# The score maxima of an attention kernel: TensorE transposes in the first batch, block transposes after it, and the reduced maximum kept in PSUM

## The chip, the core and the metric

The kernel runs on one core of a Trainium2 chip. The metric is device time in microseconds (us) of one execution; less is better. Before the change the median of three runs is 1071.49 us (1071.37 to 1074.14).

Five engines work side by side and each executes its own instructions strictly in the order written: TensorE (PE; its weight loads have a row of their own, PEld), VectorE (DVE), ScalarE (ACT), GpSimd (POOL) and SyncE (SP, which here issues most DMAs). They wait for one another by semaphores.

## The reference

Hashed attention, then a two-layer feed-forward block, all in float32.

```
q_bits = (q @ proj > 0); k_bits likewise; buckets are the 6 bits read as a number
scores = where(q_bucket == k_bucket, 0.125 * q @ k.T, -1e9)      # 4 batches x 8 heads, 768 x 768, head dim 64
scores = scores - max(scores, axis=-1)                            # the part that the change touches
attn   = exp(scores);  attn = attn / (attn.sum(-1) + 1e-9)
x      = (attn @ v) gathered to 3072 x 512
h = x @ w_in (512 x 2048);  g = s * max(h, 0)**2 + b;  out = g @ w_out (2048 x 512)
```

## The kernel before, in words

A *slot* is one chunk of 256 queries of one head: 4 batches x 8 heads x 3 chunks = 96 slots. In a slot, TensorE writes the transposed scores (keys on the partitions, queries along the free axis) into three PSUM banks, 0 to 2 in one kind of slot and 5 to 7 in another. Slots of the first batch alternate between the two sets of banks. From the 25th slot on all slots use banks 0 to 2, since banks 5 to 7 then belong to the feed-forward block (`moe`), whose matmuls (L710 and L727) fill TensorE between the attention steps. The feed-forward work is added from the last slot of the first batch on (GATE = 23), so the first batch has none of it. Instead its 32 weight tiles are decoded there (`decode`: L362 and L363 on ACT, L364 and L365 on DVE, L366, L373 and L374 on POOL). Half of the heads of the first batch are computed in plain float32 (the *exact* ones), all others from operands split into two parts.

The maximum over the keys runs across the partitions and takes this chain in every slot, `scores` from L575 to L592:

1. L575, DVE: maximum over the six key tiles, three PSUM banks to `mx` (128x256, in SBUF).
2. L577, DVE: `mx` is transposed in place in blocks of 32x32.
3. L578, DVE: maximum over each block's 32 columns, to `nmt` (128x8).
4. L582, PE: transpose of `nmt` into PSUM bank 4 (8x128).
5. L584, DVE: maximum over the four groups of 32, negated, to `qm` (8x32, in SBUF).
6. L592, DVE, the *row operation*: `qm` repeated eight times, times eight columns of the identity, to 8x256 in SBUF (`zhl` in exact heads, `bq` in the others). Both its inputs are in SBUF.
7. L601 (exact) or L603, PE, six matmuls: they add the negated maximum to the scores in PSUM. Then ACT takes exp (L608).

PSUM bank 4 is shared by this chain and by all preparation of later heads: transposes L436 and L450, hash matmuls L469 and L479 to L481, sums of v L516 and L531.

No instruction order is written by hand. The code adds steps to a `Plan`, each with its engine, a cost in us, what it reads and writes, and a priority. `Plan.order` then simulates the engines with these costs and emits each engine's instructions in the order that came out. `plan.hold(4)` keeps bank 4 for one group of steps until the last of them is done. A cost is thus a planning number: it decides what stands between two steps, not how long they take.

Of the kernel before, what the change touches and what calls it, by code (L numbers as in the profile page):

```python
# [10 lines left out]
F32 = mybir.dt.float32  # L11
# [146 lines left out]
CHAIN = 0.05  # L158
OFF = 0.4
BEHIND = 8.0  # L160
LOOK = {DVE: 0.5, ACT: 0.0, POOL: 0.0}


@with_exitstack
def lsh_attention_moe(ctx: ExitStack, tc, q, k, v, proj, w_in, w_out, s, b, out):
# [31 lines left out]
    def tile_(name, shape, dt=F32):  # L197
        return const.tile(shape, dt, name=name)
# [13 lines left out]
    def act(n, fn, r, w, pr, more=0.0):  # L212
        plan.add(ACT, 0.13 + n / 1070.0 + more, fn, r, w, pr)
# [31 lines left out]
    zhl = tile_("zhl", [P, 2, CH], F32R)  # L245
    zpb = tile_("zpb", [P, NXP, CH])
    vmn = tile_("vmn", [D, 2 * H])
    nmt = tile_("nmt", [P, NR])
    QM = tile_("qm", [NR, SQ])
    oner = tile_("oner", [P, P], F32R)  # L250
    xpb = tile_("xpb", [P, NXP, CH])
    xsb = tile_("xsb", [P, 2, CH], F32R)
# [87 lines left out]
    def decode(u, pr):  # L340
# [9 lines left out]
        def raw():  # L350
            return box["t"]
# [10 lines left out]
        act(512, lambda: nc.scalar.activation(g, raw()[:, :, 1].bitcast(F32), AF.Copy, scale=float(2.0**-112)), rk + [("pace", u % PACE)], [gk], pr)  # L362
        act(512, lambda: nc.scalar.activation(raw()[:, :, 0], raw()[:, :, 0].bitcast(U32), AF.Copy, scale=float(2.0**-29)), rk, rk, pr)  # L363
# [190 lines left out]
    def scores(i, pr):  # L554
# [8 lines left out]
        for p in range(NP_):  # L563
# [5 lines left out]
                        continue  # L569
                    nc.tensor.matmul(o, ks[0:HR + NR, 0, kt], aq[0:HR + NR, cs], start=m == 0, stop=m == 1, skip_group_check=True)  # L570
            pe(mmc(CH, 8 if exact else 2), lead, AK(x) + KK(x) if exact else AK(x, g=CG[c])  + KK(x, (0, 2, 4)), [("b", pb[p])], pr, True)
        t, tk, nm, nk = MX, "mx", nmt, "nm"

        sc = bank[:, b0:b0 + NP_].rearrange("p b (m n) -> p n b m", n=CH)
        dve(S * TPC, lambda: nc.vector.tensor_reduce(t, sc, AX.XY, ALU.max), [("b", b) for b in pb], [tk], pr, 1.75)  # L575
        m2, m2k = MX, "mx"
        dve(CH, lambda: nc.vector.transpose(out=m2, in_=t), [tk], [m2k], pr, 0.33)  # L577
        dve(CH, lambda: nc.vector.tensor_reduce(nm, m2.rearrange("p (b n) -> p b n", n=SQ), AX.X, ALU.max), [m2k], [nk], pr, 0.33)  # L578
        plan.hold(4)
        plan.soon[len(plan.steps) - 1] = plan.now[1]  # L580
# [33 lines left out]
    def values(i, pr, pieces):  # L614
# [7 lines left out]
        for p in range(NP_):  # L622
            z, y = PIECES[i][p], nhl[0] % NHL
            nhl[0] += 1
            if not exact:
                act(512, lambda z=z, y=y: nc.scalar.copy(HL[2 * y].rearrange("p (m n) -> p m n", n=CH), pairs(z)), [("e", z)], [("hl", 2 * y)], pr)  # L626
# [12 lines left out]
            for p_ in pieces[(p * len(pieces) + NP_ - 1) // NP_:((p + 1) * len(pieces) + NP_ - 1) // NP_]:  # L639
                p_(i, pr + PP)  # L640
# [194 lines left out]
```

## Time and profile before

| | before |
|---|---|
| median of three runs | 1071.49 us |
| the profiled execution | 1071.43 us |
| its span, first to last instruction | 1069.6 us |
| PE busy | 1014.5 us (95%) |
| DVE busy | 731.7 us (68%) |
| ACT busy | 672.5 us (63%) |
| POOL busy | 659.8 us (62%) |
| mean granted TensorE clock | 0.986 |

Busy time is the union of an engine's instruction spans, so a matmul stretched by a slow clock counts in full. A stage is judged by its own idle time, not by these means: the first batch (to 193 us), the three batches that share TensorE with the feed-forward block (to about 890 us), and a tail with the feed-forward block alone.

### The profile page before, as it was taken

The numbers are of one execution on the slowest core, as the hardware profiler recorded it, in microseconds if no ns is written. First come the engines' busy times: TensorE is split into PE (matmuls) and PEld (weight loads), VectorE is DVE, ScalarE is ACT, GpSimd is POOL, SyncE is SP. The second block draws the span as 40 slices with busy tenths as digits, with TensorE's granted clock in tenths as the row PEclk, the third lists the DMA queues.
The fourth block names the chain that finished last, engine by engine and source line by source line (L and its number), as shares of the span: only waits on it lengthen the run. The fifth ranks groups of instructions, "written<-read, shape, count | busy, mean of one in ns | idle before, by whom it ended". The sixth has DMA issues, their size and how long they took to land.

```text
span 1069.6 us, 18187 instructions
## 1 busy us (share of the span) xinstructions
PE 1014.5 (95%) x6614; PEld 901.3 (84%) x6614; DVE 731.7 (68%) x940; ACT 672.5 (63%) x1325; POOL 659.8 (62%) x596
## 2 busy tenths in 40 slices
PE   8988869879999999999999999999999999999998
PEld 6876657768888988888888899888899889999997
DVE  6898998967788878878788778878778863000000
ACT  4767676757766666667766766676776765333332
POOL 1656777686677667767686677767776765222221
PEclk9999998979999999999999999999999999999999
DMA  6666655412332242234143233233242211101010
GB/s 175 148 185 155 176 150 130 139 30 71 103 96 65 59 120 60 69 94 120 32 114 86 68 106 95 64 91 90 60 118 65 64 40 50 60 1 59 8 43 20
DMA packets 93681, 93.07 MB, mean 87 GB/s; under 512 B 62744, under 2 KB 66328, under 8 KB 93592
## 3 DMA queue, kind: packets, MB, share of 16 engines
q1 hardware_dynamic: 88392, 74.87, 26.2%
q10 hardware_dynamic: 5200, 17.05, 5.5%
q8 instruction: 52, 0.85, 0.3%
q14 instruction: 37, 0.30, 0.1%
HBM read 48.24 MB, written 18.87 MB: 63 GB/s over the span
## 4 chain that ended last, share of the span: by engine, by line
PE 50%; DVE 7%; ACT 2%; POOL 1%; issue 1%; DMA 1%; DVEq 0%; SPq 0%; ACTq 0%; POOLq 0%
PE bank L710 18%; PE bank L727 17%; PE bank L603 4%; PE bank L570 3%; PE bank L634 2%; PE bank L633 2%; DVE bq L592 2%; DVE mx L575 1%; DVE zpb L673 1%; PE bank L661 1%; ACT et L608 1%; PE bank L450 1%; POOL glb L718 1%; DVE zb L653 1%; DVE qm L584 0%
## 5 line engine op out<-in xcount | busy, mean ns | idle before, releaser
L627 POOL TENSOR_TENSOR hl<-et,hl 128x512 fp32r<-128x512 f32 x216 | 279.4, 1319 | 103.5 <-ACT hl L626 80.6
L710 PE MATMUL bank<-xc,w 128*128 128x256 f32 x2304 | 329.6, 284 | 0.8 <-ACT rb L715 0.8
L710 PEld LDWEIGHTS bank<-xc,w 128*128 128x128 f32 x2304 | 303.2, 191 | 7.7 <-ACT rb L715 1.2
L727 PE MATMUL bank<-w,ghb 128*128 128x512 f32 x768 | 254.9, 399 | 0.0
L718 POOL TENSOR_TENSOR glb<-rb,ghb 128x512 fp32r<-128x512 f32 x96 | 127.8, 1331 | 136.4 <-ACT ghb L717 127.5
L653 DVE TENSOR_REDUCE zb<-et 128x256 f32<-128x1536 f32 x72 | 126.1, 1752 | 75.2 <-ACT et L608 73.9
L608 ACT ACTIVATE et<-bank 128x512 f32<-128x512 f32 x240 | 132.5, 625 | 68.3 <-PE bank L603 54.5
L575 DVE TENSOR_REDUCE mx<-bank 128x256 f32<-128x1536 f32 x96 | 168.0, 1750 | 7.8 <-PE bank L570 3.8
L727 PE MATMUL bank<-w,glb 128*128 128x512 f32 x384 | 152.9, 399 | 0.0
L715 ACT ACTIVATE rb<-bank 128x512 f32<-128x512 f32 x96 | 57.2, 596 | 149.4 <-PE bank L710 148.2
L727 PEld LDWEIGHTS bank<-w,ghb 128*128 128x128 f32 x768 | 135.4, 189 | 17.9
L626 ACT CAST hl<-et 128x512 fp32r<-128x512 f32 x216 | 130.9, 663 | 0.4
L633 PE MATMUL bank<-hl,vs 128*128 128x256 f32 x432 | 116.8, 290 | 4.6 <-DVE xpb L668 4.1
L634 PE MATMUL bank<-hl,vs 128*128 128x256 f32 x432 | 115.7, 287 | 3.8 <-POOL hl L627 3.8
L570 PE MATMUL bank<-aq,ks 84*128 84x256 f32 x504 | 104.6, 299 | 0.2 <-ACT et L608 0.2
L603 PE MATMUL bank<-bq,ks 128*128 128x256 f32 x504 | 83.2, 302 | 16.5 <-DVE bq L592 16.2
L735 DVE SCALAR_TENSOR_TENSOR osb<-bank,misc,bcs 128x512 f32<-128x512 f32 x22 | 16.0, 744 | 120.7 <-PE bank L727 120.6
L603 PEld LDWEIGHTS bank<-bq,ks 128*128 128x128 f32 x504 | 67.6, 194 | 30.9 <-DVE bq L592 28.6
L634 PEld LDWEIGHTS bank<-hl,vs 128*128 128x128 f32 x432 | 83.5, 193 | 10.5 <-POOL hl L627 5.6
L633 PEld LDWEIGHTS bank<-hl,vs 128*128 128x128 f32 x432 | 83.4, 193 | 10.4 <-DVE xpb L668 4.5
L570 PEld LDWEIGHTS bank<-aq,ks 84*128 84x128 f32 x504 | 82.6, 192 | 7.9 <-ACT et L608 1.2
L666 ACT ACTIVATE xpb<-bank,vmn 64x256 f32<-64x256 f32 x96 | 44.9, 468 | 70.0 <-PE bank L634 68.6
(117 smaller groups left out, 1613.7 us busy)
## 6 DMA issues: line engine op xcount, KB each, us to landing
xd<-xsb SPq DMA_DIRECT2D x48, 256.0 KB
xc<-xd SPq DMA_DIRECT2D x48, 256.0 KB
raw<-in_moe_w_in_dram ACTq DMA_DIRECT2D x16, 512.0 KB
raw<-in_moe_w_out_dram ACTq DMA_DIRECT2D x16, 512.0 KB
nat<-in_q_dram SPq DMA_DIRECT2D x32, 192.0 KB
nat<-in_k_dram SPq DMA_DIRECT2D x32, 192.0 KB
out_dram<-osb SPq DMA_DIRECT2D x22, 256.0 KB
ks<-aq SPq DMA_DIRECT2D x28, 192.0 KB
```

Of the source, the lines that this page charges most:

```text
L570: nc.tensor.matmul(o, ks[0:HR + NR, 0, kt], aq[0:HR + NR, cs], start=m == 0, stop=m == 1, skip_group_check=True)
L575: dve(S * TPC, lambda: nc.vector.tensor_reduce(t, sc, AX.XY, ALU.max), [("b", b) for b in pb], [tk], pr, 1.75)
L603: nc.tensor.matmul(o, ks[:, 1, kt], bq[:, cs], start=False, stop=m == 1, skip_group_check=True)
L608: act(512, lambda p=p, z=z: nc.scalar.activation(et(z) if plain(i) else pairs(z), bank[:, pb[p]] if plain(i) else bank[:, pb[p]].rearrange ...
L626: act(512, lambda z=z, y=y: nc.scalar.copy(HL[2 * y].rearrange("p (m n) -> p m n", n=CH), pairs(z)), [("e", z)], [("hl", 2 * y)], pr)
L627: pool(512, lambda z=z, y=y: nc.gpsimd.tensor_tensor(HL[2 * y + 1].rearrange("p (m n) -> p m n", n=CH), pairs(z), f32(HL[2 * y]).rearrange ...
L633: nc.tensor.matmul(av, VS[x][:, kt], HL[2 * y][:, ms], start=(kt == 0), stop=False)
L634: nc.tensor.matmul(av, VS[x][:, kt], HL[2 * y + 1][:, ms], start=False, stop=(kt == NT - 1))
L653: dve(S * TPC, lambda: nc.vector.tensor_reduce(ZB, es, AX.XY, ALU.add), [("e", z) for z in range(NE)], ["zb"], pr, 1.75)
L710: nc.tensor.matmul(hp, wt[("wi", n, cc)][:, m % 2, fs], xc[:, m // 2, :], start=(cc == 0 and m == 0), stop=(cc == NC_ - 1 and m == 2))
L718: pool(2 * CH, lambda r=r, gh=gh, gl=gl: nc.gpsimd.tensor_tensor(gl, r, f32(gh), ALU.subtract), [rk, hk], [lk], MP)
L727: nc.tensor.matmul(bank[:, 6 + t, :], (gh, gh, gl)[n][:, ts], wt[("wo", f)][:, n % 2], start=(f == 0 and n == 0), stop=(f == NF - 1 and n ...
```

## The change: what it does

In slots of the first batch (`turn` false) the block transposes and the reduction behind them are replaced. TensorE transposes `mx` as two 128x128 pieces into bank 4 (L588 after the change), one DVE reduction from PSUM takes the negated maximum (L590, 128x2, into its own half of `nmt`, which was cleared once), TensorE transposes that (L592), and the row operation (L599) reads bank 4 directly; there is no `qm` step.

In the other three batches (`turn` true) steps 1 to 4 stay, but the small maximum (L595 after the change) is written to free columns of bank 4 and the row operation (L599) reads it there. In all slots the row operation now has one input in PSUM and one in SBUF, and bank 4 is held until the row operation is done.

Several planning costs are changed: the block transpose from 0.33 to 0.45 us, the reductions from 0.33 to 0.42 and 0.26 to 0.27, the row operation from 0.33 to 0.41, and 0.05 or 0.06 more for ACT's decode steps and casts. So the order of all engines changes.

```diff
+TURN = 1
-    nmt = tile_("nmt", [P, NR])
-    QM = tile_("qm", [NR, SQ])
+    nmt = tile_("nmt", [P, 2, NR])
+    nc.vector.memset(nmt, 0.0)
@@ decode
-        act(512, ... AF.Copy, scale=float(2.0**-112)), rk + [("pace", u % PACE)], [gk], pr)
+        act(512, ... AF.Copy, scale=float(2.0**-112)), rk + [("pace", u % PACE)], [gk], pr, 0.06)
...
@@ scores
-        t, tk, nm, nk = MX, "mx", nmt, "nm"
+        turn = slots[i][0] >= TURN
+        t, tk, nm, nk = MX, "mx", nmt[:, turn], ("nm", turn)
...
-        dve(CH, lambda: nc.vector.transpose(out=m2, in_=t), [tk], [m2k], pr, 0.33)
-        dve(CH, lambda: nc.vector.tensor_reduce(nm, m2.rearrange("p (b n) -> p b n", n=SQ), AX.X, ALU.max), [m2k], [nk], pr, 0.33)
+        if turn:
+            dve(CH, lambda: nc.vector.transpose(out=t, in_=t), [], [tk], pr, 0.45)
+            dve(CH, lambda: nc.vector.tensor_reduce(nm, t.rearrange("p (b n) -> p b n", n=SQ), AX.X, ALU.max), [tk], [nk], pr, 0.42)
         plan.hold(4)
         plan.soon[len(plan.steps) - 1] = plan.now[1]
+        if not turn:
+            def across():
+                for j in range(TPC):
+                    nc.tensor.transpose(out=bank[:, 4, j * P:(j + 1) * P], in_=t[:, j * P:(j + 1) * P], identity=ident)
+            pe(0.23, across, [tk], [("b", 4, "c")], pr, True)
+            dve(CH, lambda: nc.vector.tensor_reduce(nm[:, 0:TPC], bank[:, 4, 0:CH].rearrange("p (j n) -> p j n", j=TPC), AX.X, ALU.max, negate=True), [("b", 4, "c")], [nk], pr, 0.41)
         pe(0.115, lambda: nc.tensor.transpose(out=bank[0:NR, 4, 0:P], in_=nm, identity=ident), [nk], [("b", 4, "c")], pr, True)
-        qm, qk = QM, "qm"
-        dve(CH, lambda: nc.vector.tensor_reduce(qm, bank[0:NR, 4, 0:P].rearrange("b (k n) -> b n k", n=SQ), AX.X, ALU.max, negate=True), [("b", 4, "c")], [qk], pr, 0.26)
-        plan.hold(None)
+        n, o = (NR, bank[0:NR, 4, P:P + SQ]) if turn else (TPC, bank[0:NR, 4, 0:P])
+        if turn:
+            dve(CH, lambda: nc.vector.tensor_reduce(o, bank[0:NR, 4, 0:P].rearrange("b (k n) -> b n k", n=SQ), AX.X, ALU.max, negate=True), [("b", 4, "c")], [("qm", 4)], pr, 0.27)
         def rows():
-            o = qm.rearrange("p (j n) -> p j n", j=1).broadcast_to([NR, NR, SQ])
-            d = ident[0:NR, 0:NR].rearrange("p (j n) -> p j n", n=1).broadcast_to([NR, NR, SQ])
-            nc.vector.scalar_tensor_tensor(mr.rearrange("p (j n) -> p j n", j=NR), o, -FLOOR, d, ALU.min, ALU.mult)
-        dve(CH, rows, [qk], [mk], pr, 0.33)
+            d = ident[0:NR, 0:n].rearrange("p (j n) -> p j n", n=1).broadcast_to([NR, n, CH // n])
+            nc.vector.scalar_tensor_tensor(mr.rearrange("p (j n) -> p j n", j=n), o.rearrange("p (j n) -> p j n", j=1).broadcast_to([NR, n, CH // n]), -FLOOR, d, ALU.min, ALU.mult)
+        dve(CH, rows, [("b", 4, "c"), ("qm", 4)], [mk], pr, 0.41)
+        plan.hold(None)
```

What this does to the order is shown at two places. The first is TensorE in the 46th slot (second batch), from the transpose of `nmt` to the six matmuls that need the row operation. `hl` and `vs` are the attention weights and values, `xc`, `w`, `ghb` and `glb` the feed-forward operands. Before:

```order
L582 MATMUL bank<-ident,nmt 8x128
L710 MATMUL bank<-xc_2_0_2463,w_756 128x256
L710 MATMUL bank<-xc_2_1_3322,w_798 128x256 x2
L633 MATMUL bank<-hl_1595,vs_3056 128x256
L634 MATMUL bank<-hl_1607,vs_3056 128x256
L633 MATMUL bank<-hl_1595,vs_3056 128x256
L634 MATMUL bank<-hl_1607,vs_3056 128x256
L710 MATMUL bank<-xc_2_1_3322,w_798 128x256
L603 MATMUL bank<-bq_71,ks_73 128x256 x6
```

And the same place in the changed kernel, where the transpose is L592 and the six matmuls are L611:

```order
L592 MATMUL bank<-ident,nmt 8x128
L735 MATMUL bank<-w_913,ghb 128x512
L641 MATMUL bank<-hl_1593,vs_3106 128x256
L642 MATMUL bank<-hl_1602,vs_3106 128x256
L641 MATMUL bank<-hl_1593,vs_3106 128x256
L642 MATMUL bank<-hl_1602,vs_3106 128x256
L735 MATMUL bank<-w_913,glb 128x512
L718 MATMUL bank<-xc_2_0_2399,w_1044 128x256
L611 MATMUL bank<-bq_71,ks_73 128x256 x6
```

Between the transpose and the matmuls that wait stood eight matmuls of 256 columns; now there are five of 256 and two of 512 columns, one 256-column matmul's worth more.

The second place is in the first batch, the thirteenth slot. TensorE before, from the transpose of `nmt`; `eqa` and `eka` are the exact queries and keys, `nat` the raw ones of a later head:

```order
L568 MATMUL bank<-eqa,eka 128x256 x4
L582 MATMUL bank<-ident,nmt 8x128
L450 MATMUL bank<-ident,nat_66 128x128 x3
L601 MATMUL bank<-zhl,oner 128x256 x6
L631 MATMUL bank<-et,eva 128x256 x2
```

And in the changed kernel, where L588 is the transposes of `mx`, L592 that of `nmt` and L609 the matmuls that need the row operation:

```order
L588 MATMUL bank<-ident,mx 128x128 x2
L639 MATMUL bank<-ex_86,vs_210 128x256
L639 MATMUL bank<-ex_87,vs_210 128x256 x2
L569 MATMUL bank<-eqa,eka 128x256 x2
L592 MATMUL bank<-ident,nmt 8x128
L569 MATMUL bank<-eqa,eka 128x256 x2
L609 MATMUL bank<-zhl,oner 128x256 x2
L517 MATMUL bank<-misc,vs_780 64x1 x6
L609 MATMUL bank<-zhl,oner 128x256 x4
```

The chain now passes TensorE twice, with five matmuls between the two passes and two behind the second. The next head's preparation (L450) no longer stands between the transpose and the matmuls that need the row operation.

## Rows read from the trace of the kernel before

**Rows 1.** The page: span, and busy time of each engine.
```profile
span 1069.6 us, 18187 instructions
PE 1014.5 (95%) x6614; PEld 901.3 (84%) x6614; DVE 731.7 (68%) x940; ACT 672.5 (63%) x1325; POOL 659.8 (62%) x596
```

**Rows 2.** Busy time by stage: first batch, passage, three batches, tail.
```profile
core 0: us, PE busy (x) PEld busy (x) DVE busy (x) ACT busy (x) POOL busy (x), PEclk, DMA share, GB/s
16.70:193.00 176.30, 153.20 (x819) 124.81 (x818) 157.11 (x222) 121.97 (x244) 111.44 (x95) 0.96 0.59 159
193.00:260.00 67.00, 58.66 (x357) 51.36 (x356) 53.53 (x64) 43.47 (x89) 51.40 (x45) 0.87 0.28 75
260.00:890.00 630.00, 613.11 (x4253) 555.10 (x4252) 502.31 (x610) 441.75 (x888) 446.78 (x409) 1.00 0.30 82
890.00:1069.60 179.60, 176.06 (x1116) 159.11 (x1114) 10.10 (x14) 59.86 (x99) 46.85 (x39) 1.00 0.09 32
```

**Rows 3.** Who waited for whom, PE, 260 to 890 us: total, times, longest.
```profile
PE bank L603 <- DVE bq L592: 13.5, 29, 0.9
PE bank L634 <- POOL hl L627: 3.1, 5, 0.9
```

**Rows 4.** The row operation and its kin: count, shortest/median/longest ns.
```profile
L592 DVE SCALAR_TENSOR_TENSOR bq<-qm,ident x84: 411/562/1579, 60.7 to 884.8; 8x256 fp32r<-8x256 f32 x84
L592 DVE SCALAR_TENSOR_TENSOR zhl<-qm,ident x12: 411/414/1200, 20.3 to 190.9; 8x256 fp32r<-8x256 f32 x12
L365 DVE SCALAR_TENSOR_TENSOR osb<-osb,raw x32: 628/691/1668, 24.1 to 224.1; 128x512 int32<-128x512 int32 x32
L668 DVE TENSOR_TENSOR xpb<-xpb,bank x72: 422/424/427, 209.0 to 895.9; 64x256 f32<-64x256 f32 x72
L741 DVE SCALAR_TENSOR_TENSOR osb<-bank,misc,bcs x4: 476/480/487, 1065.2 to 1066.5; 128x256 f32<-128x256 f32 x4
```

**Rows 5.** Timeline, one slot of the second batch: start us, us, instruction.
```profile
433.77 0.28 DVE L584 TENSOR_REDUCE qm<-bank 8x32 f32<-8x128 f32 x1 [0.77 <-PE bank L582]
434.09 1.58 DVE L592 SCALAR_TENSOR_TENSOR bq<-qm,ident 8x256 fp32r<-8x256 f32 x1
434.13 1.26 POOL L718 TENSOR_TENSOR glb<-rb,ghb 128x512 fp32r<-128x512 f32 x1
435.72 0.98 PE L603 MATMUL bank<-bq,ks 128*128 128x256 f32 x6 [0.94 <-DVE bq L592]
```

**Rows 6.** Row operations' busy time (count) by stage: first batch, passage, three batches.
```profile
16.70:193.00 176.30, 16.14 (x24) 0.96 0.59 159
193.00:260.00 67.00, 3.80 (x6) 0.87 0.28 75
260.00:890.00 630.00, 48.86 (x66) 1.00 0.30 82
```

**Rows 7.** Groups of the whole run: busy, mean ns, idle before.
```profile
L577 DVE STREAM_TRANSPOSE mx<-mx 128x256 f32<-128x256 f32 x96 | 42.6, 444 | 3.0
L578 DVE TENSOR_REDUCE nmt<-mx 128x8 f32<-128x256 f32 x96 | 40.3, 420 | 3.3
L582 PE MATMUL bank<-ident,nmt 128*8 128x128 f32 x96 | 26.5, 276 | 6.8 <-DVE bq L454 5.5 <-DVE nmt L578 0.7 <-DVE nat L484 0.4
L584 DVE TENSOR_REDUCE qm<-bank 8x32 f32<-8x128 f32 x96 | 25.6, 267 | 30.9 <-PE bank L582 29.8
```

**Rows 8.** Timeline: three TensorE transposes in a row.
```profile
417.58 0.49 PE L450 MATMUL bank<-ident,nat 128*128 128x128 f32 x3
```

**Rows 9.** Chain that ended last: start us, us; a feed-forward run of each kind.
```profile
899.45 2.87 PE bank L710 x24
902.32 2.77 PE bank L727 x12
```

**Rows 10.** Who waited for whom, PE, first batch (16.7 to 193 us).
```profile
PE bank L582 <- DVE bq L454: 5.3, 2, 4.4
PE bank L450 <- DVE qm L584: 4.3, 7, 1.5
PE bank L436 <- DVE qm L584: 2.3, 3, 1.7
PE bank L601 <- DVE zhl L592: 2.2, 5, 0.7
PE bank L516 <- DVE qm L584: 2.1, 2, 1.3
PE bank L603 <- DVE bq L592: 2.0, 3, 0.9
```

**Rows 11.** Timeline: the 25th maximum reduction; the longest stall of the passage.
```profile
192.92 1.68 DVE L575 TENSOR_REDUCE mx<-bank 128x256 f32<-128x1536 f32 x1
226.23 0.58 PE L633 MATMUL bank<-hl,vs 128*128 128x256 f32 x1 [4.11 <-DVE xpb L668]
```

More of the change, by code (lines that the diff above doesn't have):

```diff
@@ L361, in decode @@
         plan.add(ACT, 0.1, lambda: nc.scalar.dma_start(raw(), src.rearrange("p (n t) -> p n t", t=2)), KK("a") if u < PACE else [], rk + [("pace", u % PACE)], pr - 5, 5.0)
-        act(512, lambda: nc.scalar.activation(g, raw()[:, :, 1].bitcast(F32), AF.Copy, scale=float(2.0**-112)), rk + [("pace", u % PACE)], [gk], pr)
-        act(512, lambda: nc.scalar.activation(raw()[:, :, 0], raw()[:, :, 0].bitcast(U32), AF.Copy, scale=float(2.0**-29)), rk, rk, pr)
+        act(512, lambda: nc.scalar.activation(g, raw()[:, :, 1].bitcast(F32), AF.Copy, scale=float(2.0**-112)), rk + [("pace", u % PACE)], [gk], pr, 0.06)
+        act(512, lambda: nc.scalar.activation(raw()[:, :, 0], raw()[:, :, 0].bitcast(U32), AF.Copy, scale=float(2.0**-29)), rk, rk, pr, 0.06)
         dve(256, lambda: nc.vector.tensor_scalar(raw()[:, :, 1], gi, -2**31, None, ALU.bitwise_and), [gk], rk, pr, 0.6)
@@ L571, in scores @@
             pe(mmc(CH, 8 if exact else 2), lead, AK(x) + KK(x) if exact else AK(x, g=CG[c])  + KK(x, (0, 2, 4)), [("b", pb[p])], pr, True)
-        t, tk, nm, nk = MX, "mx", nmt, "nm"
+        turn = slots[i][0] >= TURN
+        t, tk, nm, nk = MX, "mx", nmt[:, turn], ("nm", turn)
         sc = bank[:, b0:b0 + NP_].rearrange("p b (m n) -> p n b m", n=CH)
         dve(S * TPC, lambda: nc.vector.tensor_reduce(t, sc, AX.XY, ALU.max), [("b", b) for b in pb], [tk], pr, 1.75)
-        m2, m2k = MX, "mx"
@@ L577, in scores @@
-        dve(CH, lambda: nc.vector.transpose(out=m2, in_=t), [tk], [m2k], pr, 0.33)
-        dve(CH, lambda: nc.vector.tensor_reduce(nm, m2.rearrange("p (b n) -> p b n", n=SQ), AX.X, ALU.max), [m2k], [nk], pr, 0.33)
+        mk = ("mrow", y) if exact else ("mr", x, c)
+        mr = zhl[0:NR, y] if exact else bq[0:NR, cs]
+        if turn:
+            dve(CH, lambda: nc.vector.transpose(out=t, in_=t), [], [tk], pr, 0.45)
+            dve(CH, lambda: nc.vector.tensor_reduce(nm, t.rearrange("p (b n) -> p b n", n=SQ), AX.X, ALU.max), [tk], [nk], pr, 0.42)
@@ L579, in scores @@
         plan.hold(4)
         plan.soon[len(plan.steps) - 1] = plan.now[1]
-        pe(0.115, lambda: nc.tensor.transpose(out=bank[0:NR, 4, 0:P], in_=nm, identity=ident), [nk], [("b", 4, "c")], pr, True)
-        qm, qk = QM, "qm"
-        dve(CH, lambda: nc.vector.tensor_reduce(qm, bank[0:NR, 4, 0:P].rearrange("b (k n) -> b n k", n=SQ), AX.X, ALU.max, negate=True), [("b", 4, "c")], [qk], pr, 0.26)
-        plan.hold(None)
-        mk = ("mrow", y) if exact else ("mr", x, c)
-        def rows():
-            mr = zhl[0:NR, y] if exact else bq[0:NR, cs]
-            o = qm.rearrange("p (j n) -> p j n", j=1).broadcast_to([NR, NR, SQ])
-            d = ident[0:NR, 0:NR].rearrange("p (j n) -> p j n", n=1).broadcast_to([NR, NR, SQ])
-            nc.vector.scalar_tensor_tensor(mr.rearrange("p (j n) -> p j n", j=NR), o, -FLOOR, d, ALU.min, ALU.mult)
@@ new lines, in scores, with rows @@
+        pe(0.115, lambda: nc.tensor.transpose(out=bank[0:NR, 4, 0:P], in_=nm, identity=ident), [nk], [("b", 4, "c")], pr, True)
+        n, o = (NR, bank[0:NR, 4, P:P + SQ]) if turn else (TPC, bank[0:NR, 4, 0:P])
+        if turn:
+            dve(CH, lambda: nc.vector.tensor_reduce(o, bank[0:NR, 4, 0:P].rearrange("b (k n) -> b n k", n=SQ), AX.X, ALU.max, negate=True), [("b", 4, "c")], [("qm", 4)], pr, 0.27)
+        def rows():
+            d = ident[0:NR, 0:n].rearrange("p (j n) -> p j n", n=1).broadcast_to([NR, n, CH // n])
+            nc.vector.scalar_tensor_tensor(mr.rearrange("p (j n) -> p j n", j=n), o.rearrange("p (j n) -> p j n", j=1).broadcast_to([NR, n, CH // n]), -FLOOR, d, ALU.min, ALU.mult)
@@ L625, in values @@
             if not exact:
-                act(512, lambda z=z, y=y: nc.scalar.copy(HL[2 * y].rearrange("p (m n) -> p m n", n=CH), pairs(z)), [("e", z)], [("hl", 2 * y)], pr)
+                act(512, lambda z=z, y=y: nc.scalar.copy(HL[2 * y].rearrange("p (m n) -> p m n", n=CH), pairs(z)), [("e", z)], [("hl", 2 * y)], pr, 0.05)
                 pool(512, lambda z=z, y=y: nc.gpsimd.tensor_tensor(HL[2 * y + 1].rearrange("p (m n) -> p m n", n=CH), pairs(z), f32(HL[2 * y]).rearrange("p (m n) -> p m n", n=CH), ALU.subtract), [("e", z), ("hl", 2 * y)], [("hl", 2 * y + 1)], pr, 1.3)
```

## The prediction

> **What bounds the kernel now.** I read the page first: span 1069.6 us, PE busy 1014.5 us of it, DVE next with 731.7 [rows 1]. So the time is TensorE's work plus TensorE's idle time, and the question is where that idle time lies. The table by stage tells it [rows 2]. In the first batch PE is busy 153.2 of 176.3 us (23.1 idle), in the passage to 260 us 58.7 of 67.0 (8.3 idle), in the three batches beside the feed-forward block 613.1 of 630.0 (16.9 idle), and in the tail 176.1 of 179.6. The feed-forward work is a filler that TensorE always has from 260 us on: an idle microsecond that goes there comes off the end, since the tail is TensorE work without a break.
>
> Then the waits of the third stage: 13.5 of its 16.9 us of idle time are one wait, L603 for the row operation L592, 29 times, 0.9 us at the longest [rows 3]. What the row operation takes is in its list of durations: 411 ns at the shortest, 562 in the middle, 1579 at the longest, for always the same 8x256 elements [rows 4]. The timeline shows what it waits for: at 434.09 it starts, GpSimd's L718 starts at 434.13 and ends at 435.39, and the row operation ends 0.28 us after that; L603 had stood idle for 0.94 us [rows 5]. The kin in the same list split alike. L365, also with two inputs in SBUF, spreads from 628 to 1668 ns. L668 and L741, with one input in PSUM, spread by 5 and 11 ns [rows 4]. So the spread goes with two SBUF inputs beside a running GpSimd instruction. In the first batch DVE is busy 157.1 of 176.3 us, more than PE [rows 2], and its longest waits of PE are for DVE or for bank 4 that DVE holds [rows 10].
>
> **Part 1: the row operation reads PSUM, all 96 slots.** Its busy time is 16.14 + 3.80 + 48.86 = 68.8 us, 0.717 us each [rows 6]. With one PSUM input I expect no spread. From below 0.411 us, the shortest of today; from above 0.480 us, L741 with three operands at the same 256 columns; I take 0.425, since L668, with one PSUM input and 256 columns, has 0.424 [rows 4]. That makes 96 x 0.425 = 40.8 us, 28 us less on DVE (22.7 to 29.3).
>
> L668 reads PSUM and takes 13 ns more than the undisturbed row operation reading SBUF [rows 4]. [...]
>
> On the path: the saving counts where PE waits. In the third stage the row operation costs 48.86 - 66 x 0.425 = 20.8 us more than it will, 0.32 us per slot, but PE waits in 29 slots only, for 13.5 us, on average 0.47 us [rows 3, 6]. At least 29 x 0.32 = 9.2 us go, if the waits were spread like the average slot; at most all 13.5. I take 12: the slots that wait are those with the long row operation, and the order now has one more 256-column matmul in front of L611, 2.87/24 = 0.12 us [rows 9]. What is late next is the chain from the transpose itself: 0.276 for L582, 0.267 for the reduction [rows 7], 0.425 and some 0.1 of handing over are 1.07 us, against 5 x 0.12 + 2 x 0.231 = 1.06 us of matmuls in the order after [rows 9]. In the first batch the same wait is 2.2 + 2.0 us [rows 10], of which 3.5 go. Part 1 gives -12 - 3.5 = **-15.5 us** (-11 to -18).
>
> **Part 2: the small maximum written to PSUM (72 slots).** No row shows a DVE write to PSUM. From below the reduction stays at 0.267 us; from above it costs as much more as the dearest PSUM reading above, 0.48 - 0.41 = 0.07 us, 5 us of DVE in 72 slots, of which PE sees what its order does not cover. I take 0: DVE idles 128 of 630 us in the third stage [rows 2]. Bank 4 is held 0.43 us longer per slot; behind it queue the preparation steps of later heads, and PE has feed-forward matmuls to put there. If that cover is gone, 0.43 us in each of the 72 slots would be 31 us; the order above shows it is not.
>
> **Part 3: the first batch (24 slots).** DVE loses the block transpose, its reduction and the small maximum, 0.444 + 0.420 + 0.267 = 1.13 us, and gains a reduction of 128x256 from PSUM. No row shows that one; from below 0.420 as from SBUF, from above 0.48 as L741; I take 0.42, for L668 shows 13 ns for PSUM. So DVE does 0.71 x 24 = 17 us less, and with the row operation (16.14 - 24 x 0.425 = 5.9) 23 us less of its 157. PE gains 48 transposes. Three in a row take 0.49 us, the first 0.27, so each further one 0.11 [rows 8, 7]: 48 x 0.11 = +5.3 us, all inside a stage in which PE idles 23.1 us. It also gains a wait: PE's second transpose waits for the DVE reduction in the middle of the chain. Behind it on PE's queue are the scores and values of neighbouring slots, for which ACT waits. Transposes, hand-over and reduction are 0.27 + 0.11 + 0.1 + 0.42 = 0.9 us, and in the order five matmuls of the exact kind stand between; I take the wait as covered on average.
>
> What does the lighter DVE buy? Between two bounds: if DVE sets the pace, the stage shortens by the 17 us that part 1 has not counted; if PE does, it gets 5.3 us longer. PE's waits other than for the row operation that end with DVE or bank 4 are 5.3 + 4.3 + 2.3 + 2.1 = 14 us in the first batch [rows 10]. I let three quarters go, for the preparation transposes no longer stand between the transpose and L609 in the order shown, and DVE is a seventh lighter: -10.5 + 5.3 = **-5 us** (-17 to +5).
>
> **Part 4: the costs.** They move instructions and remove none. The stalls that a new order may make or remove are of the size of the 4.11 us wait for L668 [rows 11]. The granted clock was 0.87 on average in the passage with that stall and 0.96 in the first batch, and 1.00 afterwards [rows 2]; 13% of 67 us and 4% of 176 us lost at half speed are 9 + 7 = 16 us. I take 0 with 8 to either side.
>
> Sum: 1071.4 - 15.5 - 5 = **1051 us**, against the profiled execution's own 1071.43, which is 0.06 below the median of the runs.
>
> **Rivals.**
>
> *The second pass over TensorE (slower).* In the first batch each chain stands twice in PE's queue. If neither the order's matmuls cover the first pass nor the second, each slot loses the pass and the reduction, 0.38 + 0.42 = 0.8 us; 24 slots make 19, the transposes 5.3, and the preparation that waits for bank 4 (4.3 + 2.3 + 2.1 = 8.7 us today [rows 10]) doubles: +33 - 15.5, 1089 us. It decides the sign from 0.4 us exposed per slot on (15.5 - 5.3 = 10 us over 24 slots). Half-way it is 1078. For it: PE is 87% busy there and already waits for bank 4. Against: the matmuls between the two passes, and DVE's 23 us.
>
> *The row operation does not get shorter.* If it waits for something other than GpSimd's use of SBUF, or PSUM costs as much, only part 3 is left: 1066 us. For it: rows 5 show one case and not the mechanism. Against: the two kin that never spread.
>
> *The clock.* [...] The granted clock fell in both stages in which PE had stalls of over 4 us [rows 2, 10, 11]. One more loses the stall and 9 us: 1051 + 13 = 1064 us. [...]
>
> *DVE sets the pace of the first batch.* Then 23 us go there in all, with 12 in the third stage: 1071.4 - 35 = 1036 us. For it: DVE is the busiest engine there. Against: PE at 87% with 5.3 us more.
>
> **How the numbers follow.** The forecast has 0.57, the second pass 0.09, the unshortened row operation 0.08, the clock 0.11, DVE's pace 0.15. The likeliest case gives 1051. The range runs from DVE's pace, 1036, to just above the unshortened row operation, 1067; outside it lie the second pass above, and below it the half of the last case that goes further still: some 0.17 in all. About 0.3%, 3.2 us, can be told from no change here. Slower by more is the second pass alone: 0.08. Within 0.3%: the rest of it and the upper ends of the two cases at 1064 and 1066, 0.07. Faster: 0.85.
>
> **What would show it.** Right: the row operation (L599) at 0.41 to 0.48 us without a long tail; PE's idle time before L611 in the three batches under 3 us; PE idle from 260 us on under 8 us; the 25th maximum reduction, at 192.92 now [rows 11], 5 to 12 us earlier; DVE busy 40 to 50 us less. Wrong: long waits of L592 for L590 and of L609 for L599 in the first batch (second pass); a row operation still above 0.6 us (second rival); a granted clock under 0.95 in a stage (third); a first batch of 155 us or less (fourth).

## The result, and the profile after

The changed kernel takes 1038.98 us (median of four runs, 1037.88 to 1041.35) against 1071.92 us of the kernel before on the same chip: a ratio of 0.969 with an interval of 0.967 to 0.972, 33 us less. The forecast was 1051 us, with a range of 1036 to 1067. So the sign and the place of the largest term were right, and the gain was about 60% larger than forecast (33 us against 20). In all runs below, ratios are to the kernel before, run on the same chip; its medians on the chips used are 1071.9 to 1073.5 us.

The page of the profiled execution, answering to [rows 1]:

```profile
span 1036.4 us, 18211 instructions
PE 999.8 (96%) x6662; PEld 898.0 (87%) x6662; DVE 685.2 (66%) x893; ACT 673.6 (65%) x1325; POOL 654.5 (63%) x596
```

The span is 33.2 us shorter. PE's idle time, span less busy, went from 55.1 to 36.6 us, which is 18.5 of it. The other 14.7 are busy time, although PE has 48 transposes more. The same stages as in [rows 2], busy time and granted clock:

```profile
16.70:193.00 176.30, 155.37 (x875) 128.24 (x874) 137.10 (x177) 123.81 (x247) 112.25 (x97) 0.99 0.58 159
193.00:260.00 67.00, 61.59 (x416) 54.45 (x415) 50.41 (x65) 48.13 (x96) 53.11 (x46) 1.00 0.32 83
260.00:890.00 630.00, 626.89 (x4406) 576.08 (x4406) 482.89 (x609) 450.40 (x901) 453.54 (x418) 1.00 0.30 81
890.00:1036.40 146.40, 142.55 (x898) 128.23 (x896) 6.15 (x10) 46.30 (x75) 32.26 (x25) 0.99 0.11 37
```

Two things are to be seen. From 260 to 890 us PE idles 3.1 us, not 16.9. And in the first 260 us the granted clock is 0.99 and 1.00 where it was 0.96 and 0.87. What TensorE lost at half speed there (the clock of the kernel before is 0.50 from 224.8 to 241.8 us), the missing share of the clock times the stretch, was 0.04 x 176 + 0.13 x 67 = 16 us before and is 2 now.

The operations of the maximum (shortest/median/longest ns), answering to [rows 4] and [rows 7]. L599 is the row operation, L590 the reduction from PSUM in the first batch, L595 the small maximum, now written to PSUM:

```profile
L599 DVE SCALAR_TENSOR_TENSOR bq<-bank,ident x84: 349/411/414, 62.6 to 872.8; 8x256 fp32r<-8x256 f32 x84
L599 DVE SCALAR_TENSOR_TENSOR zhl<-bank,ident x12: 349/411/415, 21.0 to 187.7; 8x256 fp32r<-8x256 f32 x12
...
L590 DVE TENSOR_REDUCE nmt<-bank x24: 360/424/426, 20.1 to 185.8; 128x2 f32<-128x256 f32 x24
...
L595 DVE TENSOR_REDUCE bank<-bank x72: 223/286/288, 194.3 to 872.6; 8x32 f32<-8x128 f32 x72
```

The tail of durations up to 1579 ns is gone: no row operation is longer than 415 ns. And PE's waits of 260 to 890 us that the view lists (2.9 of the 3.1 us idle), answering to [rows 3]; the wait for the row operation is not among them any more:

```profile
PE bank L642 <- POOL hl L635: 1.3, 3, 0.6
PE bank L735 <- POOL glb L726: 0.7, 1, 0.7
PE bank L592 <- DVE bq L455: 0.4, 1, 0.4
PE bank L669 <- ACT xpb L674: 0.3, 1, 0.3
PE bank L571 <- ACT et L616: 0.2, 1, 0.2
```

In the first batch the second pass over TensorE shows as a wait of its own, L592 for L590, answering to [rows 10]; it is 2.7 us in all, and the old wait of 5.3 us for L454 (L455 after the change) is not in the list any more:

```profile
PE bank L639 <- ACT ex L616: 3.6, 7, 1.0
PE bank L571 <- DMA aq<-nat: 3.0, 3, 1.2
PE bank L451 <- DVE zhl L599: 2.8, 3, 1.6
PE bank L592 <- DVE nmt L590: 2.7, 5, 1.0
PE bank L611 <- DVE bq L599: 1.6, 3, 1.0
```

The 25th maximum reduction, answering to [rows 11], starts 2.8 us earlier than before:

```profile
190.14 1.75 DVE L577 TENSOR_REDUCE mx<-bank 128x256 f32<-128x1536 f32 x1
```

### The profile page after: what moved, and what is told of

It reads as the page before. It is cut to its first block, busy times and chain, and to the rows that moved or that the text cites. A ratio compares the mean times of both kernels' runs of the same rounds, so it can differ in the third digit from the quotient of the medians.

```text
span 1036.4 us, 18211 instructions
## 1 busy us (share of the span) xinstructions
PE 999.8 (96%) x6662; PEld 898.0 (87%) x6662; DVE 685.2 (66%) x893; ACT 673.6 (65%) x1325; POOL 654.5 (63%) x596
## 4 chain that ended last, share of the span: by engine, by line
PE 86%; POOL 4%; DMA 3%; DVE 2%; ACT 2%; issue 2%; SPq 0%; DVEq 0%; ACTq 0%; POOLq 0%
PE bank L718 26%; PE bank L735 25%; PE bank L571 5%; PE bank L611 5%; PE bank L642 5%; PE bank L641 5%; PE bank L639 4%; PE bank L569 2%; PE bank L669 2%; PE bank L451 2%; DMA aq<-nat 1%; POOL hl L635 1%; POOL osb L367 1%; DMA xd<-xsb 1%; PE bank L592 1%
## 5 line engine op out<-in xcount | busy, mean ns | idle before, releaser
L718 PE MATMUL bank<-xc,w 128*128 128x256 f32 x2304 | 337.5, 285 | 0.6 <-ACT rb L723 0.4
L726 POOL TENSOR_TENSOR glb<-rb,ghb 128x512 fp32r<-128x512 f32 x96 | 125.0, 1302 | 120.4 <-ACT ghb L725 110.8
L642 PE MATMUL bank<-hl,vs 128*128 128x256 f32 x432 | 113.7, 284 | 5.3 <-POOL hl L635 5.3
L641 PE MATMUL bank<-hl,vs 128*128 128x256 f32 x432 | 113.9, 284 | 0.0
L642 PEld LDWEIGHTS bank<-hl,vs 128*128 128x128 f32 x432 | 81.7, 189 | 13.7 <-POOL hl L635 7.8
L681 DVE RECIPROCAL zpb<-zpb 128x256 f32<-128x256 f32 x48 | 83.6, 1741 | 5.7 <-ACT zpb L672 5.6
L641 PEld LDWEIGHTS bank<-hl,vs 128*128 128x128 f32 x432 | 81.7, 189 | 6.1
L735 PEld LDWEIGHTS bank<-w,glb 128*128 128x128 f32 x384 | 72.2, 188 | 11.8 <-POOL glb L726 1.1
```

Source lines behind the costliest of these rows:

```text
L681: dve(CH, lambda: nc.vector.reciprocal(zp, zp), [], zk, pr + 20, 1.75)
L718: nc.tensor.matmul(hp, wt[("wi", n, cc)][:, m % 2, fs], xc[:, m // 2, :], start=(cc == 0 and m == 0), stop=(cc == NC_ - 1 and m == 2))
L726: pool(2 * CH, lambda r=r, gh=gh, gl=gl: nc.gpsimd.tensor_tensor(gl, r, f32(gh), ALU.subtract), [rk, hk], [lk], MP)
L735: nc.tensor.matmul(bank[:, 6 + t, :], (gh, gh, gl)[n][:, ts], wt[("wo", f)][:, n % 2], start=(f == 0 and n == 0), stop=(f == NF - 1 and n ...
```

## The experiments

Theory: in the later batches the row operation waited for GpSimd because both its inputs lay in SBUF, and PSUM frees it; in the first batch TensorE's transposes help by relieving DVE. Rivals: the gain comes from the new order and not from the place of the small maximum; the gain of the first batch is the granted clock. Three edits can be told apart: the small maximum in PSUM, the transposes on TensorE, the costs. All times are medians of four runs.

### The same order, the small maximum in SBUF

```diff
-        n, o = (NR, bank[0:NR, 4, P:P + SQ]) if turn else (TPC, bank[0:NR, 4, 0:P])
+        n, o = (NR, MX[0:NR, 0:SQ]) if turn else (TPC, bank[0:NR, 4, 0:P])
```

> The changed kernel, with every engine's order word for word the same, but in the 72 slots of the last three batches the small maximum goes to a corner of mx in SBUF and the row operation reads it there. If the row operation waits for GpSimd only when both its inputs are in SBUF, its 72 durations spread again from 0.41 to over 1.2 us with a mean of about 0.7, PE's waits of L611 for L599 come back with 10 us or more, and the time is 1050 to 1062 us. If the gain lies in the new order (one more matmul in front of L611) and not in the memory of the small maximum, the time stays within 4 us of the changed kernel's 1039. If reading PSUM is itself dearer than reading SBUF, the shortest row operations fall below the 411 ns of the changed kernel.

Measured: 1059.38 us, ratio 0.989 (0.986 to 0.992), 20 us more than the changed kernel. Every engine executes the same instructions in the same order; only the operand's memory differs. The durations of the 72 row operations, then the 24 of the first batch that still read PSUM:

```profile
L599 DVE SCALAR_TENSOR_TENSOR bq<-mx,ident x72: 411/880/1477, 197.4 to 894.2; 8x256 fp32r<-8x256 f32 x72
...
L599 DVE SCALAR_TENSOR_TENSOR zhl<-bank,ident x12: 348/408/413, 20.9 to 190.6; 8x256 fp32r<-8x256 f32 x12
L599 DVE SCALAR_TENSOR_TENSOR bq<-bank,ident x12: 349/408/413, 65.8 to 167.2; 8x256 fp32r<-8x256 f32 x12
```

The same slot in both timelines shows the mechanism by itself. Changed kernel:

```profile
369.87 0.29 DVE L595 TENSOR_REDUCE bank<-bank 8x32 f32<-8x128 f32 x1 [0.15 <-PE bank L592]
370.09 1.28 POOL L726 TENSOR_TENSOR glb<-rb,ghb 128x512 fp32r<-128x512 f32 x1
...
370.19 0.41 DVE L599 SCALAR_TENSOR_TENSOR bq<-bank,ident 8x256 fp32r<-8x256 f32 x1
...
370.99 0.88 PE L611 MATMUL bank<-bq,ks 128*128 128x256 f32 x6
```

With the small maximum in SBUF:

```profile
375.93 0.28 DVE L595 TENSOR_REDUCE mx<-bank 8x32 f32<-8x128 f32 x1 [0.18 <-PE bank L592]
376.14 1.29 POOL L726 TENSOR_TENSOR glb<-rb,ghb 128x512 fp32r<-128x512 f32 x1
...
376.24 1.46 DVE L599 SCALAR_TENSOR_TENSOR bq<-mx,ident 8x256 fp32r<-8x256 f32 x1
...
377.76 0.97 PE L611 MATMUL bank<-bq,ks 128*128 128x256 f32 x6 [0.56 <-DVE bq L599]
```

In both, the row operation starts 0.10 us after GpSimd's L726. Reading PSUM it ends in 0.41 us beside it. Reading SBUF it ends 0.27 us after L726 has ended, and PE stands. The traces show the same for every slot. Of the 72 row operations that read SBUF here, 51 took over 440 ns; each of them started while a GpSimd instruction was running and ended 269 to 277 ns after the end of one. The 21 others took 411 to 414 ns; none of them started with more than 0.13 us of a GpSimd instruction still to run, and a GpSimd instruction that began during them did not lengthen them. In the changed kernel, 65 of the 96 started with more than that still to run, and none took over 415 ns. So the theory's first half is shown, with the order excluded. Reading PSUM costs nothing more here: 411 ns is the shortest with both inputs in SBUF, and the median (349 the shortest) with one in PSUM.

The run also shows how to read the loss. PE's wait for the row operation is 9.8 us in this stage, but the run is 20 us slower:

```profile
PE bank L611 <- DVE bq L599: 9.8, 25, 0.8
```
```profile
260.00:890.00 630.00, 617.11 (x4282) 559.36 (x4281) 499.65 (x600) 442.86 (x886) 442.17 (x405) 1.00 0.30 81
```

The count says it: 4282 matmuls in these 630 us against 4406, 124 fewer at 626.89/4406 = 0.142 us each, 17.6 us. 0.142 is the mean over matmuls of all sizes, so this is an estimate. A 256-column matmul's record is 0.28 us long while the next one starts 0.12 us after it (four of L641 and L642 from 370.15 us on in the changed kernel), so the first 0.16 us of such a wait lies under the record before and counts as busy. On the weight-load row such waits are longer. Over the whole run, PE and PEld:

```profile
PEld bank L611: 24.6, 43
PE bank L611: 13.1, 31
```

### The small maximum in PSUM alone

The changed kernel with TURN = 0 (block transposes everywhere) and the old costs. That is the kernel before with the one edit, bank 4 held until the row operation is done as in the changed kernel. All seven costs are set back; one of them is shown.

```diff
-TURN = 1
+TURN = 0
-            dve(CH, lambda: nc.vector.transpose(out=t, in_=t), [], [tk], pr, 0.45)
+            dve(CH, lambda: nc.vector.transpose(out=t, in_=t), [], [tk], pr, 0.33)
...
```

> The kernel before with the small maximum in PSUM in all 96 slots, the old planning costs, and no transposes of the maxima on TensorE. By part 1 of the prediction 15.5 us (11 to 18): 1053 to 1060 us, with the row operation at 0.41 us everywhere. If the gain needs the new order, 1066 or more. If the stalls of over 4 us and the slow clock behind them go by themselves when DVE has 28 us less to do, 1045 or less.

Measured: 1056.88 us, ratio 0.986 (0.984 to 0.987), 15 us less than before, the 15.5 that part 1 of the prediction forecast. The places are not those of the forecast. In the profiled execution, at 1060.3 us the longest of the four, 260 to 890 us has 100 matmuls more than before, 14 us by 0.142 us each, where 12 were forecast; the first 260 us has 26 fewer, where a gain of 3.5 us was forecast. The clock stays low there, 0.96 and 0.82, although the longest of PE's waits in the first 260 us is now 2.4 us:

```profile
16.70:193.00 176.30, 151.80 (x817) 125.22 (x815) 150.90 (x220) 122.14 (x243) 107.97 (x94) 0.96 0.55 155
193.00:260.00 67.00, 57.74 (x333) 51.05 (x334) 50.71 (x66) 42.82 (x86) 49.81 (x45) 0.82 0.29 77
260.00:890.00 630.00, 624.77 (x4353) 569.27 (x4352) 486.09 (x614) 449.31 (x903) 452.40 (x419) 1.00 0.31 83
```

### The costs alone

The kernel before with the seven new costs and nothing else; one of them is shown.

```diff
-        dve(CH, lambda: nc.vector.transpose(out=m2, in_=t), [tk], [m2k], pr, 0.33)
+        dve(CH, lambda: nc.vector.transpose(out=m2, in_=t), [tk], [m2k], pr, 0.45)
...
```

> The kernel before with the new planning costs alone; all instructions as before, the row operation with both inputs in SBUF. By the prediction's part 4 the costs are worth 0, with 8 us to either side: 1063 to 1080 us. The rival, that the new order makes the gain by putting more matmuls in front of those that wait and by removing the two stalls of over 4 us and the slow clock behind them, expects 1045 to 1055.

Measured: 1081.91 us, ratio 1.009 (1.008 to 1.011), 10 us slower than before, and outside the intervals that both theories gave, 2 us above the upper one. Costs nearer to the traced durations did not help by themselves.

### No transposes on TensorE

```diff
-TURN = 1
+TURN = 0
```

> The changed kernel without TensorE's transposes in the first batch: block transposes on DVE in all 96 slots, the small maximum in PSUM in all, the new costs. By the prediction's part 3 the first batch's edit is worth 5 us: 1044 us. If DVE sets the pace of the first batch, 17 us are lost: about 1056. If TensorE does, its 5 us of transposes are saved: 1034.

Measured: 1053.77 us, ratio 0.984 (0.981 to 0.986), 15 us more than the changed kernel. This is near what a first batch paced by DVE would lose (1056), and not the 5 us of part 3 (1044). The clock is 0.90 in both stages, and the 25th maximum reduction comes at 206.26, 16 us later than in the changed kernel. From 260 us on nothing is lost: 4444 matmuls against 4406.

```profile
16.70:193.00 176.30, 149.98 (x767) 124.36 (x766) 138.46 (x207) 114.61 (x227) 101.80 (x88) 0.90 0.52 151
193.00:260.00 67.00, 56.09 (x327) 48.26 (x326) 54.89 (x70) 43.95 (x88) 50.38 (x45) 0.90 0.33 87
260.00:890.00 630.00, 630.00 (x4444) 580.97 (x4443) 487.38 (x618) 456.02 (x909) 453.95 (x418) 1.00 0.31 83
```
```profile
206.26 1.74 DVE L577 TENSOR_REDUCE mx<-bank 128x256 f32<-128x1536 f32 x1
```

In the same 176 us DVE is busy 138.5 us, about as long as in the changed kernel (137.1), so a full DVE is not the whole reason. The lower clock and PE's waits for the row operation (11.5 us on the weight-load row up to 206 us, at most 2.3 each) go with the longer batch; which of them makes it longer, this run does not show.

```profile
PEld bank L611 <- DVE bq L599: 11.5, 7, 2.3
```

### The old costs beside both other edits

The changed kernel, TURN = 1, with the seven old costs (as in the diff of the PSUM-alone run).

> The changed kernel with the old planning costs: TensorE's transposes in the first batch and the small maximum in PSUM, but the order made with the old costs. Adding up the single edits measured so far (small maximum in PSUM -15, costs +10 alone, transposes about -15 beside both), the old costs would be better here by up to 10: about 1030 us. If the costs only cost something where the row operation is not in PSUM or DVE is full, the time is within 4 us of 1039. If the new costs are what lets PE's matmuls cover the chain, it is 1045 or more, with PE waiting for the row operation more than the 1.6 us of the changed kernel.

Measured: 1060.37 us, ratio 0.988 (0.984 to 0.992). So the three edits do not add up. Beside the small maximum in PSUM (0.986), the transposes alone give 0.988 and the costs alone 0.984, neither distinguishable from 0.986 by its interval. Both together give 0.969, 18 us. As the third reading expected, PE waits longer for the row operation than in the changed kernel, 8.9 us in all on the weight-load row against 2.9. Of the 21 us to the changed kernel, 42 matmuls or 6 us lie in 260 to 890 us, where the granted clock is 1.00 in both; the rest lies in the first 260 us, which has 113 matmuls fewer. Its stages:

```profile
16.70:193.00 176.30, 156.27 (x840) 126.91 (x839) 133.56 (x168) 118.79 (x237) 111.94 (x94) 0.95 0.53 151
193.00:260.00 67.00, 57.45 (x338) 49.91 (x337) 47.80 (x60) 40.78 (x82) 44.59 (x39) 0.87 0.31 84
260.00:890.00 630.00, 626.62 (x4364) 570.24 (x4363) 494.27 (x623) 453.78 (x912) 456.12 (x424) 1.00 0.31 83
```

### Transposes everywhere

```diff
-TURN = 1
+TURN = 4
```

> The changed kernel with TensorE's transposes of the maxima in all 96 slots. In the last three batches TensorE has no idle time to take: 72 x 2 x 0.11 = 16 us more work, of which nothing is hidden, and a second wait in the chain: 1055 us or more. If DVE's 51 us less work matters more there, 1039 or less.

Measured: 1056.45 us, ratio 0.985 (0.981 to 0.989), 17 us more than the changed kernel for 144 more transposes, 0.11 us each: 16 us. From 260 to 890 us, where PE of the changed kernel idles 3.1 of 630 us, the added work counts in full, and DVE's relief (632 us busy instead of 685) shows no gain.

### Other orders of the same instructions

Three runs move one cost each, so that only the order changes: the row operation 0.45, the row operation 0.43, PE's two transposes 0.27; a fourth the maximum over six tiles, 1.78.

```diff
-        dve(CH, rows, [("b", 4, "c"), ("qm", 4)], [mk], pr, 0.41)
+        dve(CH, rows, [("b", 4, "c"), ("qm", 4)], [mk], pr, 0.45)
```

> The changed kernel with one planning cost moved, the row operation's from 0.41 to 0.45 us; every instruction as in the changed kernel, in another order. It measures how far the time moves with the order alone. If the planning costs' effect is mostly the accident of where stalls fall in the first 260 us, the time moves by 5 us or more in either direction. If the order is robust, it stays within 3 us of 1039.

> The changed kernel with the row operation's planning cost at 0.43 us instead of 0.41; the same instructions in another order. With the run at 0.45 us (1044.6, slow clock for 38 us of the first 260) it asks whether the time among orders of the same instructions goes with how long the granted clock is at its lower level and how long TensorE stands still. If it does: 1036 to 1048 us, near 1038 when the clock is low for under 10 us and near 1045 when it is for over 30. If the time moves without either, the order costs something else.

> The changed kernel with the planning cost of TensorE's two transposes of mx at 0.27 us instead of 0.23; the same instructions in another order. Expected as for the row operation's cost: 1036 to 1048 us, by the length of the slow clock. Should it come out under 1036, the changed kernel's order is not the best of its neighbours.

> The changed kernel with the planning cost of the maximum over six tiles at 1.78 us instead of 1.75; the same instructions in another order. Expected as for the two others: 1036 to 1048 us, by the length of the slow clock in the first 260 us.

Measured: 1044.57 us, ratio 0.974 (0.971 to 0.976); 1037.50, 0.970 (0.964 to 0.976); 1039.58, 0.970 (0.968 to 0.972); 1035.05, 0.966 (0.963 to 0.968). The slow neighbour has the slow clock in the passage, 0.80:

```profile
193.00:260.00 67.00, 57.00 (x325) 49.87 (x324) 50.22 (x62) 41.37 (x84) 48.43 (x44) 0.80 0.29 77
```

The executions whose profiles these are, 1047.0 and 1038.2 us, differ by 8.8 us with the same instructions in two orders, while the time lost at half speed in the first 260 us differs by 0.03 x 176 + 0.20 x 67 - 2 = 17 us. So between orders the clock goes with the time, but not microsecond by microsecond. Within one order it nearly does. The four executions of the order with 0.43 are 1032.0 and 1032.5 us at a mean granted clock of 0.996, 1042.5 at 0.987 and 1045.3 at 0.984: none lies near the median of 1037.5. From 0.996 to 0.984, the missing share of the clock grows by 0.012 x 1040 = 12.5 us, and the time grows by 13. What makes the clock fall in one of them and not in another, no run shows. The order with 1.78 is the fastest kernel measured, below the 1036 to 1048 us expected, but its interval and that of the changed kernel overlap, so no gain over it is claimed.

### Four stalls

```diff
+STALL = (36, 48, 60, 72)
...
-            dve(CH, lambda: nc.vector.tensor_tensor(xh, xh, av[D:P], ALU.add), [ak], xk, pr, 0.42)
+            def add():
+                if i in STALL:
+                    for _ in range(3):
+                        nc.vector.tensor_reduce(misc[:, 6:7], ident.rearrange("p (o n) -> p o n", o=1).broadcast_to([P, 14, P]), AX.XY, ALU.max)
+                nc.vector.tensor_tensor(xh, xh, av[D:P], ALU.add)
+            dve(CH, add, [ak], xk, pr, 0.42)
```

> The changed kernel, order as before, with three extra DVE reductions of about 1.9 us each put in front of the addition L676 in four slots of the last three batches (37th, 49th, 61st and 73rd), results to a spare column. Each holds up PE's next matmul into bank 3 by up to 5 us, like the wait for L668 at 222 us in the kernel before. If a stall costs only itself, the time grows by at most 4 x 5 = 20 us and the granted clock stays at 1.00. If the clock falls behind each and stays low for as long as it did there (17 us, half lost), it grows by about 4 x (4 + 8) = 48 us. If DVE's delay is hidden, it grows by under 5.

Measured: 1064.59 us, ratio 0.993 (0.990 to 0.996), 25.6 us more than the changed kernel, 6.4 per stall. The first of the four, and the clock around it:

```profile
322.74 6.10 DVE L680 TENSOR_REDUCE misc<-ident 128x1 f32<-128x1792 f32 x3
...
329.35 0.80 PE L670 MATMUL bank<-zhl,oner 128*128 128x256 f32 x2 [4.59 <-DVE xpb L681]
```
```profile
260.00:324.00 64.00, 62.67 (x441) 57.02 (x440) 50.94 (x65) 42.35 (x87) 46.64 (x44) 1.00 0.31 84
324.00:336.00 12.00, 7.41 (x33) 6.29 (x33) 10.79 (x11) 6.59 (x13) 5.54 (x6) 0.72 0.25 58
327.00:329.35 2.35, 0.00 (x1) 0.00 (x1) 2.32 (x3) 0.00 (x0) 0.00 (x0) 0.51 0.59 151
329.35:333.80 4.45, 4.45 (x18) 4.17 (x19) 3.41 (x4) 3.32 (x7) 2.61 (x3) 0.50 0.10 17
336.00:360.00 24.00, 24.00 (x174) 22.23 (x173) 15.68 (x24) 15.72 (x33) 13.61 (x12) 1.00 0.20 46
```

With a stall of 4.6 us the clock fell: 0.72 over 12 us, which is 3.4 us lost. Of these, 1.2 us lie in the stall itself, where nothing could have run, and 2.2 behind it, where matmuls ran at half speed. The four stalls are 4.5 to 4.6 us each. The time lies between the two theories: if the stalls count in full (18 us), what is beyond them, 7 us, is 1.8 per stall, near the 2.2 of the first.

### DVE's load in the first batch

```diff
         def rows():
...
+            if not turn:
+                nc.vector.tensor_reduce(misc[:, 6:7], ident.rearrange("p (o n) -> p o n", o=1).broadcast_to([P, 5, P]), AX.XY, ALU.max)
```

> The changed kernel, order as before, with one extra DVE reduction of 640 elements (about 0.73 us, result to a spare column) behind each of the 24 row operations of the first batch: DVE gets back the 17 us that the transposes on TensorE took from it, while the chain of the maximum stays as short as it is. If DVE's load sets the pace of the first batch, the 25th maximum reduction, at 190.1 us now, comes at 200 or later and the time is 1049 to 1056 us. If the length of the chain, with the stalls of over 1.5 us and the slow clock behind them, made the difference between 206 us without the transposes and 190 with them, it comes before 194 and the time is under 1043.

Measured: 1045.24 us, ratio 0.974 (0.971 to 0.977), 6 us more than the changed kernel. The load is 0.80 us each, and the 25th maximum reduction comes at 197.10, 7 us later:

```profile
L601 DVE TENSOR_REDUCE misc<-ident 128x1 f32<-128x640 f32 x23 | 18.3, 796 | 0.0
```
```profile
197.10 1.75 DVE L577 TENSOR_REDUCE mx<-bank 128x256 f32<-128x1536 f32 x1
```

Neither theory had it: of 19 us of DVE work 7 show. If load that is added costs what load that is taken away gains, DVE's load is a part of the first batch's pace, between a third and a half of the 16 us that the transposes bring beside the new costs, and not the whole. The granted clock is lower here too, 0.97 in the first batch and 0.95 in the passage, so this run does not part the load from the clock.

## Why the prediction was right, point by point

**The bound and the wait: right.** The third stage lost its time to the row operation's wait for GpSimd. The run with an unchanged order shows it, 20 us for 72 slots; the rival that the operation would not get shorter is out. One of the two kin named as evidence was none: L741 runs from 1065 us on, where no GpSimd instruction runs (the last ends at 1063.9 us). L668 was.

**The signs.** Of the five signs for a right forecast four came: the row operation without a tail, no listed wait of L611 in the three batches, 7.0 us of PE idle time from 260 us on (3.1 and 3.9), DVE 46.5 us less busy. The fifth, the 25th maximum reduction 5 to 12 us earlier, did not: it came 2.8 us earlier.

**Part 1, the row operation: mechanism right, two sizes off.** Its duration was put at 0.425 us and is 0.411 in the middle. The 13 ns allowed for the PSUM input after L668 do not show: 411 ns, the shortest of before with both inputs in SBUF [rows 4], is the median with one in PSUM. The third stage was put at 12 us; with the order held fixed it is 20 for 72 slots. The step that failed there is the upper bound, "at most all 13.5". It took PE's waits from the matmul records, whose tail hides 0.16 us of a wait. On the weight-load row the same wait before the change is 23.8 us and not 13.5:

```profile
PEld bank L603 <- DVE bq L592: 23.8, 42, 1.1
```

In 260 to 890 us the matmuls done by the end are the better measure: 4253 before [rows 2], 4406 after, 153 at 0.142 us, 22 us. So 10 of the 12 us that the forecast lacked lie in this stage. Alone, planned with the old costs and in all 96 slots, the edit gave 15 us. That the sum agrees with the forecast is in part luck: 14 us came in the third stage, and in the first 260 us, where 3.5 were forecast, the profiled execution lost some, with a lower clock in the passage than before (0.82 against 0.87).

**Part 2, the small maximum to PSUM: right.** Its mean is 274 ns, against 267 before [rows 7], and in 260 to 890 us no wait for bank 4 behind it is worth a row.

**Part 3, the first batch: the sum too small, and its signs mistaken for one edit's.** -5 us was forecast, "5 to 12 us earlier" for the 25th maximum reduction. Measured: 2.8 us earlier than before, but 16 earlier than without the transposes at the same costs, and 15 us in the time. The costs and the transposes are not separate terms: the costs alone leave the first batch with fewer matmuls done by 193 us (773 against 819). The cover for the second pass held: PE waits 2.7 us for L590 in all, 0.11 us per slot against the 0.4 from which that rival would have decided the sign. (Its half-way price of 1078 us does not follow from its terms: half of its 33 us gives 1072.) PE's added work, 5 us, found room there: 875 matmuls instead of 819 in the same 176.3 us, 48 of the 56 being the transposes. The run with transposes everywhere shows their price of 0.11 us where there is no room. The rest of the gain came in the passage, 59 matmuls or 8 us, with its clock at 1.00. The time of 1039 us is near the 1036 of the rival in which DVE sets the pace, but not by its mechanism: that wanted 23 us in the first batch and 12 in the third stage.

**Part 4, the costs: wrong.** "I take 0 with 8 to either side" was the mis-sized term. Alone the costs make the kernel 10 us slower; beside the small maximum in PSUM they are not distinguishable from nothing; beside that and the transposes they are worth 21 us (1060.4 to 1039.0). In the last case the third stage gives 6 us of it, and in the first 260 us the time lost at half speed goes from 0.05 x 176 + 0.13 x 67 = 17.5 us to 2. The forecast kept the 16 us lost at half speed before as they were. But the clock is not most of the 21 us: the fastest execution with the old costs, 1054.5 us at a mean clock of 0.992, is still 13 to 15 us behind the changed kernel's two at 0.993 (1039.8 and 1041.4).

**The clock rival: it had the right quantity and the wrong sign.** The stalls of over 4 us went (the longest of PE's listed waits from 16.7 to 260 us is 1.8 us now), and most of the slow clock with them: 0.99 and 1.00 in the two stages, although the first has 48 transposes more. Such stalls are not its only companions, though: with the small maximum in PSUM alone no wait of PE in the first 260 us is over 2.4 us, and the clock in the passage is 0.82.

**What stays open.** How the 18 us that transposes and costs bring together divide into DVE's load, PE's stalls and the clock is not settled. DVE's load accounts for at most about 6 by the last run. The granted clock in the first 260 us is lower than the changed kernel's in every kernel that gets less done there. Executions of one order at two clocks (0.43) show the time lost at half speed paid nearly in full, two orders (0.41 and 0.45) only half of it. No run set the clock by itself, and why it falls in one execution of an order and not in another stays open.

## What to carry to other kernels

Where one instruction of fixed size spreads in duration, compare its shortest with its mean and look which engine ends just before the long ones: moving one of two SBUF inputs to PSUM took the spread from 411 to 1579 ns down to 349 to 415, worth 20 us here. Judge the waits of an engine whose records overlap (here 0.28 us long, 0.12 us apart) by the instructions it got done in a fixed stretch, not by its idle time alone. And where a planner orders the work, hold the order fixed for one edit and move the costs for another, since two edits that, beside the first, could not be told from nothing apart were worth 18 us together here. Before a few us are put down to an order, compare executions of one order: those of the order with 0.43 lie 13 us apart.

## What the runs showed of the hardware that had not been expected

- Reading PSUM was not dearer than SBUF for the row operation (411 ns, the shortest with both inputs in SBUF and the median with one in PSUM), nor for the reduction of 128x256: a mean of 418 ns from PSUM (L590) against 420 from SBUF [rows 7].
- The row operation with two SBUF inputs, started with more than 0.13 us of a GpSimd instruction still to run, took until 269 to 277 ns after that one's end (1.46 us instead of 0.41 in the slot shown), in 51 of 51 cases of the run in the same order.
- In the first of four stalls of TensorE of 4.6 us among busy matmuls, the granted clock fell to half (0.51 in the last 2.35 us of the stall, 0.50 in the 4.45 us behind it). The four cost 6.4 us each in all.
- The same instructions in the same order took from 1032.0 us at a mean granted clock of 0.996 to 1045.3 us at 0.984 in four executions (the order with 0.43).
